# Inverse twiddle tables in quarters, the first layer norm's statistics inside inverse stage 1, two PSUM pools in inverse stage 2, and a new order of the front tables

## The chip, the cores and the metric

The kernel runs on one core of a Trainium2 chip. A core has a matrix engine (TensorE, in the profile PE, with its weight loads as PEld), VectorE (DVE), ScalarE (ACT), GpSimd (POOL) and SyncE (SP, which here only issues transfers). Every engine executes its own instructions in the order of the program; semaphores tie the engines together. SBUF is the working memory, PSUM the eight banks into which TensorE writes. The metric is the device time of one execution in microseconds (us); lower is better.

## The reference

Only what matters here: a causal long convolution with gating in front of a two-layer MLP, both with a layer norm ahead and a residual. S is 2048, D 512, DFF 1376; inputs and output are bf16.

```python
def _A_ref(q, k, v, shift_k, ssm_k, ssm_D):
    ...                                        # 4-tap causal filter of k, times v
    kv = k_shift * v
    kv_f = rfft(pad(kv, 2 * S)); kf_f = rfft(pad(ssm_k, 2 * S))
    y = irfft(kv_f * kf_f)[:S].astype(bfloat16)
    y = y + kv * ssm_D
    return q * y

x = A_q
h = x + _A_ref(_layernorm(x), A_k, A_v, A_shift_k, A_ssm_k, A_ssm_D)
h2 = h + relu(_layernorm(h) @ w1) @ w2
```

## The kernel before

The Fourier transforms are products with tables on TensorE, in two stages each way, with twiddle factors folded into the tables. The tables are made on the chip: an iota gives integers, `_turns` (L42) multiplies them by a column, adds an offset and takes the result modulo a power of two with an AND (two VectorE instructions), and a Sin on ScalarE makes the factor. The order of instructions on each engine is that of the program text (`manual_schedule`, L84); there is no scheduler.

The stages, one after another:

- *Front* (L94 to L193). The token-side inputs come by transposing transfers from SP. GpSimd makes the iotas, VectorE the turns and the diagonal tap weights `wdiag` (L172), ScalarE the Sins (`table`, L175). `c2s`, `c2c`, `c2n` are the tables of forward stage 2; `dre`, `dim` (L245, L275) those of inverse stage 1, from `dsc` (L243).
- *Forward stage 1* (L235 to L272). `to_rows` transposes the filter's rows on TensorE into PSUM, and copies alternate between ScalarE and VectorE; then eight rounds of `stage1` (small matmuls with `f1_hi`, `f1_lo`) and two `taps` each.
- *Forward stage 2, products* (L288 to L347). `spectrum_k`, then `product` and `finish`.
- *Inverse stage 1* (L394 to L408). Thirty-two steps `b`, each four matmuls of 128x256 into one of eight PSUM buffers, copied to `bp` by ScalarE or VectorE after the string in L404. Beside it run the transfers of the tokens `xh` (L356), `w1`, `w2`, and the inverse twiddles `ecore`: `ec_turns` in four parts at b = 0, 3, 10, 17 (GpSimd iota, two turns pairs on VectorE), `ec_sins` at b = 4, 12, 20, 28.
- *Inverse stage 2* (`inv2`, L419). Quarter q of the tokens uses `ecore` at n2 = 16a + 4q + l4, so that with `ecore` in four contiguous parts every quarter needs all four parts. Its matmuls are 32x32 tiles in fp32, each in two passes. The results go from PSUM tile `pz` to `zt` by ScalarE copies (L436).
- *Gate and second layer norm* (`gate`, L469; statistics, reciprocal root, normalisation on VectorE; the root for quarter 0 on ScalarE with Sqrt, L442, later ones on GpSimd, L446).
- *MLP.* Quarter 0 is transposed on TensorE (`transposes`, L517, PSUM `pt`, ScalarE copy to `hlnT`), the others by transposing transfers (L486). `mlp1` (L488) takes eleven groups of four matmuls into three PSUM buffers `ps1m`, each closed by a Relu on ScalarE; `mlp2` (L502) accumulates eleven matmuls and adds `xh` on VectorE.

At the seam between inverse stage 2 and the MLP the program text is L524 to L537: statistics and norm of quarter 0, then `inv2` and `gate` by halves of quarters 0 and 1 out of a pool `psZ0` of two `pz` buffers (all eight banks), then that pool is closed and `psT`, `psM`, `psZ` take its banks.

Of the kernel before, what the change touches and what calls it, by code (L numbers as in the profile page):

```python
# [56 lines left out]
def kernel(  # L57
# [25 lines left out]
    pl = _Pools(tc)  # L83
# [47 lines left out]
    def _sin(out, turns, M, neg=False):  # L131

        nc.scalar.activation(out=out, in_=turns, func=ACT.Sin, scale=(-TURN if neg else TURN) / M,
                             bias=(pbias if neg else nbias)[:])
# [10 lines left out]
    n2i = early.tile([P, 1], I32, name="n2i")  # L145
    for s in range(0, P, 64):
        nc.gpsimd.iota(n2i[s:s + 64, :], pattern=[[0, 1]], base=0, channel_multiplier=1)
    r2 = early.tile([P, 32, 64], I32, name="w_r")
    nc.gpsimd.iota(r2[:], pattern=[[2, 32], [128, 64]], base=1, channel_multiplier=0)
    r3 = early.tile([P, 64], I32, name="dm_r")  # L150
    nc.gpsimd.iota(r3[:], pattern=[[1, 64]], base=0, channel_multiplier=0)
    n1c = early.tile([P, 1], F32, name="n1c")
    n2c = early.tile([P, 1], F32, name="n2c")
    nc.vector.tensor_copy(out=n1c[:], in_=n1i[:])
# [7 lines left out]
    _sin(f1v[:, 0], t1[:, 0:32].rearrange("p (o k) -> p o k", o=8), 128)  # L162
    _sin(f1v[:, 1], t1[:, 32:64].rearrange("p (o k) -> p o k", o=8), 128, neg=True)


    cc = wp.tile([P, 32, P], F32R, name="c2c")
    cs = wp.tile([P, 32, P], F32R, name="c2s")
    cn = wp.tile([P, 32, P], F32R, name="c2n")
    tsn = early.tile([P, 32, 64], I32, name="w_ts")
    _turns(nc, tsn[:], r2[:], n2c[:], 8192, False)  # L170
    for rg in range(DC):
        nc.vector.tensor_tensor(out=wdiag[:, rg, :, :], in0=ident[:].unsqueeze(1).to_broadcast([P, KS, P]),  # L172
                                in1=wsh[:, rg, :].unsqueeze(2).to_broadcast([P, KS, P]), op=ALU.mult)

    def table(dst, turns, ks=slice(0, 32)):  # L175
        for dp in range(2):
# [1 line left out]
                                 scale=hsc[:, dp:dp + 1], bias=hbi[:, dp:dp + 1])  # L178

    table(cs, tsn)  # L180
# [6 lines left out]
    _turns(nc, r2[:], r2[:], n2c[:], 8192, True)  # L187
    dtab = consts.tile([P, 8, DC, 8], BF16, name="dtab")
    nc.gpsimd.tensor_copy(out=dtab[:], in_=d0[:].rearrange("p r (o g) -> p o r g", g=8))
    for h in range(4):  # L190
# [10 lines left out]
    def copy(eng, o, i):  # L201
        if eng == "A":
            nc.scalar.copy(out=o, in_=i)  # L203
        else:
            nc.vector.tensor_copy(out=o, in_=i)  # L205
# [31 lines left out]
    for q in range(8):  # L237
        to_rows(skv, q, kfl, "DADADADA"[q])

    t3 = early.tile([P, 2, 64], I32, name="dm_t")  # L240
    _turns(nc, t3[:, 0, :], r3[:], n2c[:], 64, True)
    _turns(nc, t3[:, 1, :], r3[:], n2c[:], 64, False)
    dsc = early.tile([P, 2, 64], F32, name="dm_f")  # L243
    _sin(dsc[:], t3[:], 64)
# [107 lines left out]

    late = pl.push("late", side="right")
    xh = late.tile([P, NT, D], BF16, name="xh")
    for a, src in enumerate(_tokens(x_d, 0, NT)):
        nc.sync.dma_start(out=xh[32 * a:32 * a + 32, :, :].rearrange("p t d -> p (t d)"), in_=src)  # L356
    w1 = late.tile([P, DC, DFF], BF16, name="w1")
    w2 = late.tile([P, NFC, D], BF16, name="w2")
    nc.sync.dma_start(out=w1[:], in_=B_w1.rearrange("(c p) f -> p c f", p=P))
# [18 lines left out]
    nc.vector.tensor_copy(out=k1o[:], in_=k1i[:])  # L378
    ect = {}

    def ec_turns(h):
        r4 = tmpc.tile([P, 16, 32], I32, tag="ec_r", name="ec_r", bufs=4)
        nc.gpsimd.iota(r4[:], pattern=[[1, 16], [64, 32]], base=16 * h, channel_multiplier=0)
        for quarter in (True, False):
            t = tmpc.tile([P, 16, 32], I32, tag=f"ec_t{quarter}", name="ec_t", bufs=2)
            _turns(nc, t[:], r4[:], k1o[:], 8192, quarter)
            ect[h, quarter] = t

    def ec_sins(h):
        hs = slice(16 * h, 16 * h + 16)  # L390
        _sin(ecore[:, 0, hs, :], ect[h, True][:], 8192)
        _sin(ecore[:, 1, hs, :], ect[h, False][:], 8192, neg=True)

    ec_turns(0)  # L394
    bp = slotA.tile([P, 64, 2, 2, 64], F32, tag="A", name="bp")
    for b in range(32):
        ps = psum.tile([P, 2, 2 * P], F32, tag="ps", name="psi1")
        m0 = 16 * (b % 4) + 2 * (b // 4)
        for i in range(2):
            m = 2 * b + i  # L400
            for c, d in ((0, dre), (1, dim)):
                nc.tensor.matmul(out=ps[:, i, :], lhsT=kf[:, c, 4 * m:4 * m + 4, :].rearrange("p r k -> p (r k)"),  # L402
                                 rhs=d[:].rearrange("p a b -> p (a b)"), start=(c == 0), stop=(c == 1))
        copy("ADAADADA"[b % 8], bp[:, m0:m0 + 2, :, :, :].rearrange("p g a b c -> p g (a b c)"), ps[:])  # L404
        if b in (3, 10, 17):
            ec_turns((b + 4) // 7)
        if b in (4, 12, 20, 28):
            ec_sins((b - 4) // 8)  # L408
    pl.pop("tmpc")
    pl.pop("slotB")  # L410
    pl.pop("psI")


    pzp = pl.push("psZ0", bufs=2, space=PSUM)
    ep = pl.push("ep", bufs=2)
    hp = pl.push("hp", bufs=2)
    zts, hlnTs, h1s = {}, {}, {}

    def inv2(q, l4s=(0, 1, 2, 3), between=None):  # L419
        pz = pzp.tile([P, 4, 4, P], F32, tag="pz", name="pz")  # L420
        for l4 in l4s:
            for rho in range(2):
                for a in range(4):
                    n2 = 16 * a + 4 * q + l4
                    for r4 in range(4):
                        rows = slice(32 * r4, 32 * r4 + 32)
                        rhs = bp[rows, :, rho, :, n2].rearrange("p (r g) d -> p r d g", r=DC)
                        nc.tensor.matmul(out=pz[32 * a:32 * a + 32, r4, l4, :], lhsT=ecore[rows, rho, n2, :], rhs=rhs,  # L428
                                         start=(rho == 0), stop=(rho == 1), tile_position=(32 * r4, 32 * a),
                                         skip_group_check=True)  # L430
            if between is not None:
                between(l4)
        if q not in zts:
            zts[q] = hp.tile([P, 4, D], BF16, tag="zt", name="zt")
        for l4 in l4s:
            nc.scalar.copy(out=zts[q][:, l4, :].rearrange("p (m r) -> p m r", r=4),  # L436
                           in_=pz[:, :, l4, :].rearrange("p r m -> p m r"))
# [10 lines left out]
    def stats(mv, ts):  # L448
        for t in ts:
            nc.vector.bn_stats(out=st[:, t % 4, :], in_=xh[:, t, :])  # L450
        for t in ts:
            nc.vector.bn_aggr(out=mv[:, t, :], in_=st[:, t % 4, :])  # L452
# [6 lines left out]
    def four(q):  # L459
        return [4 * q + i for i in range(4)]  # L460

    def ln1(q, on_act=False):
        stats(mv1, four(q))
        rstd(mv1, rstd1, four(q), on_act)
        qln = ep.tile([P, 4, D], BF16, tag="qln", name="qln")
        norm(qln, mv1, rstd1, four(q))
        return qln

    def gate(q, ts, qln, hln, on_act=False):  # L469
        for t in ts:  # L470
# [52 lines left out]

    qln = ln1(0, on_act=True)  # L524
    hln = new_rows(0)
    for ts in ([0, 1], [2, 3]):
        inv2(0, ts)
        gate(0, ts, qln, hln, on_act=True)
    for ts in ([0, 1], [2, 3]):
        inv2(1, ts)  # L530
    pl.pop("psZ0")
    ptp = pl.push("psT", bufs=1, space=PSUM)
    psum = pl.push("psM", bufs=3, space=PSUM)
    pzp = pl.push("psZ", bufs=1, space=PSUM)
# [7 lines left out]
    inv2(3, between=lambda i: mlp2(4 + i))  # L542
    chain(3, ln1(3))
    for sc in (2, 3):
        mlp1(sc)
# [33 lines left out]
```

## Time and profile before

| | |
|---|---|
| median of 5 executions | 234.16 us (234.05 to 234.85) |
| the profiled execution, its own time | 234.16 us |
| its span, first to last instruction | 232.4 us |
| mean granted TensorE clock | 0.97 |
| inverse stage 1 starts, first psi matmul | 101.83 us |
| inverse stage 2 starts, first pz matmul | 118.78 us |
| the first MLP matmul starts | 135.44 us |
| half clock in between | 130.5 to 140.8 us |

The span is 1.76 us shorter than the execution's own time. A line of a timeline gives the start in us, the length in us, the engine, the line of code, the operation with its operands, and in brackets how long the engine was idle before it and what released it. A line of the chain of waits gives start, length and what the end of the kernel hung on at that moment. "issue" is idle time for which the profile shows no wait.

### The profile page before, as it was taken

What the parts mean: (1) busy time and instruction counts of PE and PEld (TensorE: products, weight loads), DVE (VectorE), ACT (ScalarE), POOL (GpSimd) and SP (SyncE); (2) the same over time, 40 slices, a digit from 0 to 9 for tenths busy, and PEclk for the clock granted to TensorE, in tenths of its full rate; (3) what the DMA queues carried; (4) which work ended last, traced back from release to release, by engine and by line L of the source; (5) the groups of instructions that cost most, each with busy time, mean ns of one, the idle gap of its engine ahead of it and who ended that gap; (6) DMA issues with size and microseconds to landing.
All of it is one profiled execution on the core that took longest, in us unless ns stands there. A gap on an engine that the chain in (4) does not pass through costs nothing.

```text
span 232.4 us, 7243 instructions
## 1 busy us (share of the span) xinstructions
PE 204.9 (88%) x3092; PEld 143.0 (62%) x3111; DVE 156.1 (67%) x307; ACT 133.9 (58%) x252; POOL 58.4 (25%) x85
## 2 busy tenths in 40 slices
PE   0287998999988999989988689999999999989992
PEld 0284544989978999969975458744454544434451
DVE  6996989689987999959989976021595247740031
ACT  3765988678885888879973447502560056206500
POOL 6099500000016999970000022000102002200000
PEclk9997999999999999999999758999999999999999
DMA  5999920000000000059970000401101420042111
GB/s 183 293 223 182 173 61 4 0 4 3 6 3 3 1 0 0 3 109 212 292 242 3 6 0 9 84 25 41 29 3 29 82 65 13 0 96 60 28 45 45
DMA packets 30383, 15.45 MB, mean 67 GB/s; under 512 B 25648, under 2 KB 29200, under 8 KB 30224
## 3 DMA queue, kind: packets, MB, share of 16 engines
q1 hardware_dynamic: 29616, 14.87, 27.7%
q8 instruction: 24, 0.39, 0.7%
q10 hardware_dynamic: 736, 0.13, 0.3%
q14 instruction: 7, 0.06, 0.1%
HBM read 7.08 MB, written 2.10 MB: 40 GB/s over the span
## 4 chain that ended last, share of the span: by engine, by line
PE 56%; DVE 7%; ACT 2%; issue 1%; DMA 1%; DVEq 0%; SPq 0%; ACTq 0%
PE ps1m L498 18%; PE ps2m L510 15%; PE psi L402 7%; PE psy L338 5%; PE pz L428 5%; DVE st L450 3%; PE u L229 3%; PE u L231 3%; ACT kf L340 1%; DMA hlnT<-hln 1%; PE pt L521 1%; DVE t L328 1%; DVE hln L456 1%; DVE xh L473 1%; DVE qln L471 1%
## 5 line engine op out<-in xcount | busy, mean ns | idle before, releaser
L498 PE MATMUL ps1m<-hlnT,w 128*128 128x512 bf16 (+3 forms) x219 | 41.2, 351 | 2.3 <-ACT hlnT L522 1.2
L500 ACT ACTIVATE h1T<-ps1m 128x512 bf16<-128x512 f32 (+3 forms) x55 | 27.9, 511 | 25.3 <-PE ps1m L498 24.5
L512 DVE TENSOR_TENSOR o<-ps2m,xh 128x512 bf16<-128x512 f32 (+1 forms) x17 | 11.1, 658 | 45.7 <-PE ps2m L510 45.1
L510 PE MATMUL ps2m<-w,h1T 128*128 128x512 bf16 (+3 forms) x177 | 38.9, 366 | 0.7 <-issue 0.3
L498 PEld LDWEIGHTS <-w 128*128 128x128 bf16 (+1 forms) x220 | 22.9, 105 | 20.0 <-issue 2.8
L510 PEld LDWEIGHTS <-h1T 128*128 128x128 bf16 (+1 forms) x187 | 17.6, 98 | 21.2 <-issue 3.1
L328 DVE TENSOR_TENSOR t<-u,kf 128x704 fp32r<-128x704 f32 x32 | 26.7, 886 | 3.7 <-ACT usb L324 3.6
L328 POOL TENSOR_TENSOR t<-usb,kf 128x320 fp32r<-128x320 f32 x32 | 28.1, 915 | 2.1 <-ACT usb L324 1.7
L428 PE MATMUL pz<-bp,ecore 32*32 32x128 f32 x1024 | 23.0, 384 | 3.0 <-issue 2.0
L436 ACT CAST zt<-pz 128x512 bf16<-128x512 f32 x16 | 8.4, 591 | 26.9 <-PE pz L428 26.9
L445 POOL TENSOR_SCALAR rstd<-mv 128x4 f32<-128x4 f32 x6 | 1.4, 230 | 89.2 <-DVE mv L452 89.2
L428 PEld LDWEIGHTS pz<-bp,ecore 32*32 32x32 f32 x1024 | 14.6, 105 | 10.6 <-issue 6.5
L203 ACT CAST a<-ps 128x512 fp32r<-128x512 f32 x37 | 19.6, 591 | 2.3 <-PE ps L214 2.3
L450 DVE BATCH_NORM_STATS2 st<-xh 128x6 f32<-128x512 bf16 x32 | 19.8, 677 | 0.0
L205 DVE CAST a<-ps 128x512 fp32r<-128x512 f32 x27 | 17.6, 687 | 2.8 <-PE ps L214 2.8
L340 ACT CAST kf<-psy 128x512 fp32r<-128x512 f32 x32 | 18.3, 639 | 1.5
L402 PE MATMUL psi<-dre,kf 128*128 128x256 f32 x64 | 15.8, 288 | 0.8 <-ACT kf L340 0.8
L260 PE MATMUL pkv<-kT,wdiag 128*128 128x512 bf16 x56 | 15.7, 396 | 0.6 <-issue 0.2
L338 PE MATMUL psy<-t,ipos 128*128 128x512 f32 x48 | 15.8, 391 | 0.0
L198 PE MATMUL pst<-ident,sk 128*128 128x128 bf16 x64 | 6.6, 291 | 10.0 <-DMA sk<-in_A_ssm_k_dram 10.0
L402 PE MATMUL psi<-dim,kf 128*128 128x256 f32 x64 | 15.4, 283 | 0.0
L402 PEld LDWEIGHTS psi<-dre,kf 128*128 128x128 f32 x64 | 12.2, 191 | 1.6 <-ACT kf L340 1.3
(107 smaller groups left out, 386.2 us busy)
## 6 DMA issues: line engine op xcount, KB each, us to landing
sk<-in_A_ssm_k_dram SPq DMA_DIRECT2D x1, 2048.0 KB, 8.7
xh<-in_A_q_dram SPq DMA_DIRECT2D x4, 512.0 KB, 8.3
out_dram<-o SPq DMA_DIRECT2D x60, 32.0 KB, 1.6
w<-in_B_w_dram SPq DMA_DIRECT2D x1, 1376.0 KB, 15.4
w<-in_B_w_dram SPq DMA_DIRECT2D x1, 1280.0 KB, 18.4
hlnT<-hln SPq DMA_TRANSPOSE x12, 2.5
w<-in_B_w_dram SPq DMA_DIRECT2D x1, 96.0 KB, 18.1
d<-in_A_ssm_D_dram ACTq DMA_DIRECT2D x2, 32.0 KB, 5.8
```

The source lines that it names most:

```text
L203: nc.scalar.copy(out=o, in_=i)
L205: nc.vector.tensor_copy(out=o, in_=i)
L260: nc.tensor.matmul(out=ps[:], lhsT=wdiag[:, rg, j, :], rhs=kT[c][:, rg, 16 - j:CH + 16 - j], start=(j == 0), stop=(j == KS - 1))
L328: eng.tensor_tensor(out=t[:, :, j, :], in0=in0.unsqueeze(1).to_broadcast([P, 2, n, 2]), in1=kfr[:, :, j, ks], op=ALU.mult)
L338: nc.tensor.matmul(out=psy[:], lhsT=m_[:], rhs=t_.rearrange("p j k -> p (j k)"), start=first, stop=not first)
L340: nc.scalar.copy(out=kf[:, s, :, 2 * kp:2 * kp + 2], in_=psy[:].rearrange("p (j k) -> p j k", k=2))
L402: nc.tensor.matmul(out=ps[:, i, :], lhsT=kf[:, c, 4 * m:4 * m + 4, :].rearrange("p r k -> p (r k)"), rhs=d[:].rearrange("p a b -> p (a b)" ...
L428: nc.tensor.matmul(out=pz[32 * a:32 * a + 32, r4, l4, :], lhsT=ecore[rows, rho, n2, :], rhs=rhs, start=(rho == 0), stop=(rho == 1), tile_p ...
L450: nc.vector.bn_stats(out=st[:, t % 4, :], in_=xh[:, t, :])
L498: nc.tensor.matmul(out=ps1[:fsz, :], lhsT=w1[:, c, fc * P:fc * P + fsz], rhs=hlnTs[sc][:, c, part], start=(c == 0), stop=(c == DC - 1))
L500: nc.scalar.activation(out=h1s[sc][:fsz, fc, part], in_=ps1[:fsz, :], func=ACT.Relu)
L510: nc.tensor.matmul(out=ps2[:], lhsT=h1s[sc][:ksz, fc, i * P:(i + 1) * P], rhs=w2[:ksz, fc, ds], start=(fc == 0), stop=(fc == NFC - 1))
```

## The change

Five edits:

- *Front.* The small iota of the `dm` table comes before the large one; the `dm` turns and Sin move from after the filter's transposes to before the large turns; the `wdiag` products go from VectorE to GpSimd, ahead of `dtab` and `c2n`; the second large turns pair comes ahead of the Sins of `c2s` in the text.
- *Token loads.* Tiles 0 to 3 come in four transfers of their own, then tiles 4 to 15 in four.
- *Inverse twiddles.* The parts are now the quarters that `inv2` uses. Multiply and add are one GpSimd instruction per table and quarter, all issued ahead of inverse stage 1; the ANDs stay on VectorE. Quarters 0 and 1 get their ANDs and Sins at b = 8 and 16, quarters 2 and 3 after the first transposes of the MLP, ahead of the first Relu.
- *First layer norm.* The statistics of tiles 0 to 3 are taken tile by tile at b = 19, 22, 25, 28. The engines of the last two of every eight copies are exchanged.
- *Inverse stage 2.* Two pools of one `pz` each, of four banks. The copies to `zt` are a function of their own. The last pair of copies of quarter 1 stands after the first transposes; `psT` and `psM` take the banks of `psZA`.

```diff
+    r3 = early.tile([P, 64], I32, name="dm_r")
+    nc.gpsimd.iota(r3[:], pattern=[[1, 64]], base=0, channel_multiplier=0)
     r2 = early.tile([P, 32, 64], I32, name="w_r")
     nc.gpsimd.iota(r2[:], pattern=[[2, 32], [128, 64]], base=1, channel_multiplier=0)
-    r3 = early.tile([P, 64], I32, name="dm_r")
-    nc.gpsimd.iota(r3[:], pattern=[[1, 64]], base=0, channel_multiplier=0)
...
+    t3 = early.tile([P, 2, 64], I32, name="dm_t")
+    _turns(nc, t3[:, 0, :], r3[:], n2c[:], 64, True)
+    _turns(nc, t3[:, 1, :], r3[:], n2c[:], 64, False)
+    dsc = early.tile([P, 2, 64], F32, name="dm_f")
+    _sin(dsc[:], t3[:], 64)
...
-    for rg in range(DC):
-        nc.vector.tensor_tensor(out=wdiag[:, rg, :, :], in0=ident[:].unsqueeze(1).to_broadcast([P, KS, P]),
-                                in1=wsh[:, rg, :].unsqueeze(2).to_broadcast([P, KS, P]), op=ALU.mult)
...
     _turns(nc, r2[:], r2[:], n2c[:], 8192, True)
...
+    table(cs, tsn)
+    for rg in range(DC):
+        nc.gpsimd.tensor_tensor(out=wdiag[:, rg, :, :], in0=ident[:].unsqueeze(1).to_broadcast([P, KS, P]),
+                                in1=wsh[:, rg, :].unsqueeze(2).to_broadcast([P, KS, P]), op=ALU.mult)
...
-    for a, src in enumerate(_tokens(x_d, 0, NT)):
-        nc.sync.dma_start(out=xh[32 * a:32 * a + 32, :, :].rearrange("p t d -> p (t d)"), in_=src)
+    for ts in (slice(0, 4), slice(4, NT)):
+        for a, src in enumerate(_tokens(x_d, ts.start, ts.stop - ts.start)):
+            nc.sync.dma_start(out=xh[32 * a:32 * a + 32, ts, :].rearrange("p t d -> p (t d)"), in_=src)
...
+    def ec_product(q):
+        r4 = tmpc.tile([P, 4, 4, 32], I32, tag="ec_r", name="ec_r", bufs=2)
+        nc.gpsimd.iota(r4[:], pattern=[[16, 4], [1, 4], [64, 32]], base=4 * q, channel_multiplier=0)
+        ect[q] = [tmpc.tile([P, 4, 4, 32], I32, tag=f"ec_t{c}", name="ec_t", bufs=4) for c in range(2)]
+        for c in range(2):
+            nc.gpsimd.tensor_scalar(out=ect[q][c][:], in0=r4[:], scalar1=k1o[:], scalar2=(6144.0, 4096.0)[c],
+                                    op0=ALU.mult, op1=ALU.add)
+
+    def ec_table(q):
+        for c in range(2):
+            nc.vector.tensor_single_scalar(out=ect[q][c][:], in_=ect[q][c][:], scalar=8191, op=ALU.bitwise_and)
+        for c in range(2):
+            _sin(ecore[:, c].rearrange("p (a q l) n -> p q a l n", a=4, l=4)[:, q], ect[q][c][:], 8192, neg=c == 1)
+
+    def row_stats(mv, t):
+        nc.vector.bn_stats(out=st[:, t % 4, :], in_=xh[:, t, :])
+        nc.vector.bn_aggr(out=mv[:, t, :], in_=st[:, t % 4, :])
...
-        copy("ADAADADA"[b % 8], bp[:, m0:m0 + 2, :, :, :].rearrange("p g a b c -> p g (a b c)"), ps[:])
-        if b in (3, 10, 17):
-            ec_turns((b + 4) // 7)
-        if b in (4, 12, 20, 28):
-            ec_sins((b - 4) // 8)
+        copy("ADAADAAD"[b % 8], bp[:, m0:m0 + 2, :, :, :].rearrange("p g a b c -> p g (a b c)"), ps[:])
+        if b in (8, 16):
+            ec_table(b // 8 - 1)
+        if b in (19, 22, 25, 28):
+            row_stats(mv1, (b - 19) // 3)
...
-    pzp = pl.push("psZ0", bufs=2, space=PSUM)
+    pzB = pl.push("psZB", space=PSUM)
+    pzA = pl.push("psZA", space=PSUM)
...
-        stats(mv1, four(q))
+        if not on_act:
+            stats(mv1, four(q))
...
-    for ts in ([0, 1], [2, 3]):
-        inv2(0, ts)
-        gate(0, ts, qln, hln, on_act=True)
-    for ts in ([0, 1], [2, 3]):
-        inv2(1, ts)
-    pl.pop("psZ0")
+    t01, t23 = (0, 1), (2, 3)
+    inv2_copy(0, inv2(0, t01, pool=pzA), t01)
+    inv2_copy(0, inv2(0, t23, pool=pzB), t23)
+    gate(0, t01, qln, hln, on_act=True)
+    inv2_copy(1, inv2(1, t01, pool=pzA), t01)
+    gate(0, t23, qln, hln, on_act=True)
+    pz = inv2(1, t23, pool=pzB)
+    pl.pop("psZA")
     ptp = pl.push("psT", bufs=1, space=PSUM)
     psum = pl.push("psM", bufs=3, space=PSUM)
-    pzp = pl.push("psZ", bufs=1, space=PSUM)
     transposes(0, hln)
+    inv2_copy(1, pz, t23)
+    ec_table(2)
+    ec_table(3)
     mlp1(0, slice(0, 2 * P), lambda: transposes(2, hln))
...
-    inv2(2, between=mlp2)
+    inv2_copy(2, inv2(2, between=mlp2))
```

More of the change, by code (lines that the diff above doesn't have):

```diff
@@ L170 @@
     _turns(nc, tsn[:], r2[:], n2c[:], 8192, False)
-    for rg in range(DC):
-        nc.vector.tensor_tensor(out=wdiag[:, rg, :, :], in0=ident[:].unsqueeze(1).to_broadcast([P, KS, P]),
-                                in1=wsh[:, rg, :].unsqueeze(2).to_broadcast([P, KS, P]), op=ALU.mult)
-    def table(dst, turns, ks=slice(0, 32)):
-        for dp in range(2):
-            nc.scalar.activation(out=dst[:, ks, 64 * dp:64 * dp + 64], in_=turns[:, ks, :], func=ACT.Sin,
-                                 scale=hsc[:, dp:dp + 1], bias=hbi[:, dp:dp + 1])
-    table(cs, tsn)
     f1hi = consts.tile([P, 64], BF16, name="f1_hi")
@@ L187, with table @@
     _turns(nc, r2[:], r2[:], n2c[:], 8192, True)
+    def table(dst, turns, ks=slice(0, 32)):
+        for dp in range(2):
+            nc.scalar.activation(out=dst[:, ks, 64 * dp:64 * dp + 64], in_=turns[:, ks, :], func=ACT.Sin,
+                                 scale=hsc[:, dp:dp + 1], bias=hbi[:, dp:dp + 1])
+    table(cs, tsn)
+    for rg in range(DC):
+        nc.gpsimd.tensor_tensor(out=wdiag[:, rg, :, :], in0=ident[:].unsqueeze(1).to_broadcast([P, KS, P]),
+                                in1=wsh[:, rg, :].unsqueeze(2).to_broadcast([P, KS, P]), op=ALU.mult)
     dtab = consts.tile([P, 8, DC, 8], BF16, name="dtab")
@@ L238 @@
         to_rows(skv, q, kfl, "DADADADA"[q])
[L240 to L244, printed above, removed]
     dre = consts.tile([P, 2, P], F32R, name="dre")
@@ L379 @@
     ect = {}
[L381 to L394, printed above, removed]
+    def ec_product(q):
[13 more added lines that the diff above has]
+        nc.vector.bn_aggr(out=mv[:, t, :], in_=st[:, t % 4, :])
+    for q in range(4):
+        ec_product(q)
     bp = slotA.tile([P, 64, 2, 2, 64], F32, tag="A", name="bp")
@@ L403 @@
                                  rhs=d[:].rearrange("p a b -> p (a b)"), start=(c == 0), stop=(c == 1))
-        copy("ADAADADA"[b % 8], bp[:, m0:m0 + 2, :, :, :].rearrange("p g a b c -> p g (a b c)"), ps[:])
-        if b in (3, 10, 17):
-            ec_turns((b + 4) // 7)
-        if b in (4, 12, 20, 28):
-            ec_sins((b - 4) // 8)
-    pl.pop("tmpc")
+        copy("ADAADAAD"[b % 8], bp[:, m0:m0 + 2, :, :, :].rearrange("p g a b c -> p g (a b c)"), ps[:])
[3 more added lines that the diff above has]
+            row_stats(mv1, (b - 19) // 3)
     pl.pop("slotB")
     pl.pop("psI")
-    pzp = pl.push("psZ0", bufs=2, space=PSUM)
+    pzB = pl.push("psZB", space=PSUM)
+    pzA = pl.push("psZA", space=PSUM)
     ep = pl.push("ep", bufs=2)
@@ L417, with inv2 @@
     zts, hlnTs, h1s = {}, {}, {}
-    def inv2(q, l4s=(0, 1, 2, 3), between=None):
-        pz = pzp.tile([P, 4, 4, P], F32, tag="pz", name="pz")
+    def inv2(q, l4s=(0, 1, 2, 3), between=None, pool=None):
+        pz = (pool or pzB).tile([P, 4, 4, P], F32, tag="pz", name="pz")
         for l4 in l4s:
@@ L432, in inv2, with inv2_copy @@
                 between(l4)
+        return pz
+    def inv2_copy(q, pz, l4s=(0, 1, 2, 3)):
         if q not in zts:
@@ L538 @@
     chain(1, ln1(1))
-    inv2(2, between=mlp2)
+    inv2_copy(2, inv2(2, between=mlp2))
     chain(2, ln1(2))
     mlp1(1)
-    inv2(3, between=lambda i: mlp2(4 + i))
+    inv2_copy(3, inv2(3, between=lambda i: mlp2(4 + i)))
     chain(3, ln1(3))
```

## The prediction

> **What bounds the kernel now.** I read the shares first, then the chain of waits in order of time, then one engine's timeline for each stretch that the change touches.
>
> ```profile
> PE 204.9 (88%) x3092; PEld 143.0 (62%) x3111; DVE 156.1 (67%) x307; ACT 133.9 (58%) x252; POOL 58.4 (25%) x85
> ```
>
> PE leads by far, but the mean hides the stretches without it. The chain of waits (start, length, what) shows the longest:
>
> ```profile
> 117.99 2.46 DVE st L450 x4
> ...
> 130.87 2.39 DVE st L450 x4
> 133.28 1.02 PE pt L521 x8
> 134.38 1.02 ACT hlnT L522
> 135.44 4.42 PE ps1m L498 x20
> 139.87 0.85 PE pt L521 x8
> 140.72 7.66 PE ps1m L498 x68
> 148.38 1.39 PE pz L428 x62
> ```
>
> From 117.5 to 135.4 us the chain runs through the layer norm and the gate on DVE, then transposes, a copy and the first MLP. From 148.4 on it is PE almost to the end, so a delay or gain before 148.4 passes through one for one. PE's own timeline says that DVE is not alone:
>
> ```profile
> 118.78 4.43 PE L428 MATMUL pz<-bp,ecore 32*32 32x128 f32 x210 [0.96 <-ACT bp L203]
> 123.61 2.75 PE L428 MATMUL pz<-bp,ecore 32*32 32x128 f32 x128 [0.40 <-issue]
> 126.90 2.75 PE L428 MATMUL pz<-bp,ecore 32*32 32x128 f32 x127 [0.54 <-issue]
> 130.73 1.38 PE L428 MATMUL pz<-bp,ecore 32*32 32x128 f32 x47 [1.08 <-issue]
> 133.28 1.01 PE L521 MATMUL pt<-ident,hln 128*128 128x128 bf16 x8 [1.16 <-DVE st L450]
> ```
>
> Call the start of inverse stage 2 S (118.78). Its 512 records break every 128 at "issue", not at a tile's border, and 16 KB packets of the instruction queue land about 1 us after each restart: PE waits for its own instructions. These matmuls and their order stay, so I keep their length, S to S+13.3, whatever DVE does. The wait before pt is named after DVE; ACT's timeline shows the true one, two zt copies that end at 133.22 in the PSUM which psT takes over:
>
> ```profile
> 132.15 1.07 ACT L436 CAST zt<-pz 128x512 bf16<-128x512 f32 x2 [1.29 <-PE pz L428]
> 134.38 1.01 ACT L522 COPY hlnT<-pt 128x1024 bf16<-128x1024 bf16 x1 [1.15 <-PE pt L521]
> 136.49 0.38 ACT L500 ACTIVATE h1T<-ps1m 128x256 bf16<-128x256 f32 x1 [1.10 <-PE ps1m L498]
> ```
>
> ACT is idle after that, so the first Relu costs the MLP nothing. The windows (slice, its length, busy us and count of PE, PEld, DVE, ACT and POOL, then the granted clock) show the clock: half from 130.5 to 140.8 us, which is why 20 matmuls of 256 columns take 4.42 us (0.88 for a group of four) and the later 68 take 7.66 (0.45).
>
> ```profile
> 129.00:130.00 1.00, 0.65 (x31) 0.20 (x17) 0.64 (x4) 0.39 (x2) 0.00 (x0) 1.00 0.00 0
> 131.00:132.00 1.00, 1.00 (x47) 0.54 (x18) 1.00 (x3) 0.00 (x0) 0.00 (x0) 0.50 0.08 16
> 141.00:142.00 1.00, 1.00 (x11) 0.90 (x10) 0.73 (x5) 1.00 (x3) 0.18 (x1) 1.00 0.00 0
> ```
>
> The prices that I use, from the groups:
>
> ```profile
> L192 POOL TENSOR_SCALAR c2n<-c2s 128x1024 fp32r<-128x1024 f32 x4 | 11.3, 2844 | 1.0 <-ACT c2s L177 1.0
> L133 ACT ACTIVATE ecore<-ec_t,nbias 128x512 f32<-128x512 int32 x4 | 3.0, 742 | 0.0
> L442 ACT ACT_TABLE_LOAD x1 | 1.3, 1283 | 0.0
> ```
>
> **What the Trainium skill says.** "ScalarE: Activation LUTs", section "What ACT_TABLE_LOAD costs": 1283 ns for a switch of table set, and some 1380 ns of drain behind it. The trace agrees on 1283; the drain it can't show, since ACT waited for DVE after both loads. "TensorE: Matmul & The Clock Gate", "What's actually happening": half or full clock is granted by windows of 3.4 us of PE activity. Agrees: the half clock lasted 10.24 us, three windows; a window some 79% busy (17.9 to 21.3) brought the clock back, one 65% busy (133.9 to 137.4) did not. "SBUF — State Buffer", "Who interferes with whom": a VectorE operation in a 2-port mode and a GpSimd one exclude each other for a whole instruction. Agrees only in part: VectorE's 128x2048 AND took 2.02 us beside a GpSimd c2n product and 1.23 without, slower but not shut out for that product's 3.06.
>
> **The change, part by part.**
>
> *Front.* VectorE loses wdiag (2.49 us) and makes the small dm turns first (0.9). GpSimd gains four wdiag products; nearest is its 128x320 product at 0.915 us, so 512 elements are 1.46 each, 5.9 in all, from 4.6 to 10.5 us, beside VectorE's w_ts pair. With the 2.02/1.23 slowdown w_ts ends near 10.4 instead of 7.5; ScalarE's c2s (4.2) then ends at 14.6 instead of 11.7 and its four kfl copies (3.8 back to back) at 18.4; before they waited for PE and ended at 17.7. VectorE's second table ends near 13.4, and its kfl copies at 18.0 instead of 18.4. PE's stage 1 began at 18.59, behind VectorE; now near 18.4, behind ScalarE. It runs at half clock there, so I take -0.1. Best is 17.7 (PE's last transpose plus a copy): -0.9. If each small VectorE operation waits out a whole product, as the 32-element f1 turn did beside the 2048-element iota (1.94 us against 0.23), c2s slips to 18.7 and stage 1 to 22.7: +4. c2n moves from 23 to 26-30 us, and is wanted at 46: nothing.
>
> *Inverse stage 1.* PE needs 128 matmuls by 0.12 from 101.83, to 117.6. ScalarE loses four Sins (4 by 0.64), which had made it end at 118.73: it now ends by 117.6. VectorE loses eight turns pairs (8.2 us) and gains four ANDs and four row statistics (0.68+0.15 each). GpSimd gains eight products: by L192 1.4 us for 512 elements, with a 0.68 iota per quarter: quarters are ready at 105.3, 108.8, 112.3, 115.8. The first AND is due at 106.2, the third at 110.4, after b=15: no wait. From there VectorE has two ANDs at 0.8 (GpSimd is busy beside them; 0.43 alone), six copies by 0.62, four statistics by 0.83: 8.6, to 119.0. So VectorE takes ScalarE's place and S becomes 118.3 to 119.1; I take +0.1. The product is multiply and add on integers, which no row shows: below 1.4 I see no reason; at twice that (2.8, two passes) the second quarter is ready at 114.4, behind it stand VectorE's copies and ScalarE's Sins, PE runs out of PSUM at b=25, and S is 122.2: +3.5.
>
> The token loads are split in two, four more SP issues by 0.44 us: w1 and w2 slip by 1.8 and are wanted at 135 and 150. The first quarter is wanted at 111. Nothing.
>
> *Inverse stage 2 and the MLP's start.* Statistics of quarter 0 leave (2.46+0.36 on VectorE). But PE can't use it: S+13.3 stands by instruction supply, and hln of tiles 0-1 is due at S+8.4. VectorE's gate waits for ScalarE, which now copies zt of tiles 2-3 (PE ends them at S+6.1) before the rstd: 0.7 later, hidden. With psZA freed by an earlier copy, pt no longer waits for the last zt (1.16): transposes S+13.4 to 14.4, copy to S+15.5, first ps1m at S+15.5 instead of S+16.66. That is the gain, -1.15.
>
> Behind that copy ScalarE now has, in its order of program: two zt (1.0), a table load (1.28), four Sins (3 by 0.64 + 0.7 = 2.6), and only then the first Relu: S+20.4 to S+20.75. Their ANDs are done by S+14.2, so ScalarE is the late one. psM has three buffers: PE does three groups (2.65 at half clock, to S+18.15) and stands until S+20.8. Before, its fourth group began at S+19.3. The gain is gone and 1.5 us are lost.
>
> The stall also spoils the clock: 2.65 us without PE in S+18.15 to 20.8. If windows lie as in this trace (borders at S+18.6, 22.0, 25.4), the first full one ends at S+25.4, not S+22.0. From S+20.8: two groups at 0.88, transposes 0.85, 2.2 groups more by 25.4, then 14.8 groups by 0.45: S+32.05. Before: 148.38, or S+29.6. So +2.4. Windows run freely: clock back at 23.4 gives +1.5, at 26.8 +3.2; the drain behind the table load would add up to 1.4. Without any half clock it is 20.8 + 19 by 0.45 + 0.5 = S+29.9: +0.3.
>
> *Sum.* -0.1 + 0.1 + 2.4 = +2.4 on the profiled execution's 234.16 us (span 232.4), which is also the median: 236.5.
>
> **Rivals.**
> A, the forecast, ScalarE's backlog before the first Relu: 236.5.
> B, faster: the grant of the clock. If PE is not at half clock when the MLP restarts, the stall is nearly paid by the earlier start (+0.3), and what ScalarE is spared in stage 1 (-0.5, with ANDs at 0.43) and the front (-0.5) remain: 233.5. It decides at a clock back before S+21. For it: transposes now follow pz at once. Against it: a 2.65 us hole in which a window must fall below 79%.
> C, slower still: the integer products on GpSimd take over 2.2 us and hold stage 1: 234.16 + 2.4 + up to 3.5, say 239. For it: GpSimd's rate in L192 is already 2.7 ns an element. Against: it streamed that one in a single pass.
> D: the port in the front, VectorE shut out by wdiag: 240. For it the f1 turn; against it the AND at 2.02.
> E: gains and stall cancel (clock back at 23.4, S at 118.3, stage 1 of the front at 17.7): 234.2.
>
> **Numbers.** A 0.51, B 0.17, C 0.18, D 0.08, E 0.06. So faster by over 0.2% (0.47 us, about what a measurement here can tell) 0.17, within it 0.06, slower 0.77. The range: below to B's 233.5, above to C and D, 240.0. A's own range is 235.2 to 238.2.
>
> **What would show it.** ScalarE's timeline: table load and four Sins between the hlnT copy and the first Relu, PE idle some 2.7 us after its twelfth ps1m matmul; half clock until about S+25; pt within 0.2 us of the last pz. In stage 1 VectorE, not ScalarE, releases the first pz. GpSimd's products near 1.4 us. The front's stage 1 near 18.4. I am wrong if the first Relu isn't held, if the half clock ends as early as before, or if S moves by over 1 us.

## The result, and the profile after

| | before | after |
|---|---|---|
| median of the runs | 234.26 us | 236.74 us (234.01 to 238.32, 26 runs) |
| ratio, 95% interval | | 1.0079 (1.0057 to 1.010) |
| profiled execution, its own time | 234.16 us | 237.71 us |
| its span, mean granted clock | 232.4 us, 0.971 | 235.9 us, 0.964 |
| start of forward stage 1 on PE | 18.59 | 19.27 |
| start of inverse stage 1 | 101.83 | 104.48 |
| start of inverse stage 2, S | 118.78 | 120.97 |
| first MLP matmul | S+16.66 | S+15.07 |
| end of the first MLP part | S+29.53 | S+30.66 |

The medians differ by 2.48 us (1.06%); the ratios, here and below, leave out slow runs, more than 1.5% above the fastest of their kernel (ten of after's), while the medians are of all runs. The profiled executions differ by 3.55 us: after's profile is one of its longer executions, so the stretches below are compared one by one. How much of a run goes at half clock varies, and time follows it: after's runs lie between 234.01 us at a mean clock of 0.993 and 238.32 at 0.954.

After's page, first lines of the shares (engine, busy us and share of the span, instructions): PE has done the same work, VectorE has lost 12 instructions and GpSimd gained 12.

```profile
PE 205.4 (87%) x3092; PEld 143.9 (61%) x3111; DVE 152.6 (65%) x295; ACT 135.1 (57%) x253; POOL 69.3 (29%) x97
```

After's chain of waits at the seam (start, length, what the end hung on; pieces under 0.1 us are left out):

```profile
132.95 1.38 PE pz L436 x44
134.32 0.58 PE pt L533 x8
134.98 1.01 ACT hlnT L534
135.99 0.98 ACT zt L447 x2
136.99 1.28 ACT L133
138.28 2.56 ACT ecore L133 x4
140.84 0.28 ACT h1T L512
141.16 1.86 PE ps1m L510 x8
143.02 0.85 PE pt L533 x8
143.88 7.82 PE ps1m L510 x68
151.70 1.39 PE pz L436 x62
```

Before, this stretch of the chain was VectorE's statistics, the transposes, one copy, and from then on PE alone. Now VectorE has left it, pt follows pz at once, and for 6.2 us the end hangs on ScalarE: hlnT copy, two zt copies, the table load (L133 without a tile), four Sins, the first Relu. PE's timeline of after shows what that costs (in brackets idle time and its releaser):

```profile
134.26 0.63 PE L533 MATMUL pt<-ident,hln 128*128 128x128 bf16 x8
136.04 1.47 PE L510 MATMUL ps1m<-hlnT,w 128*128 128x256 bf16 x12 [1.16 <-ACT hlnT L534]
141.16 1.86 PE L510 MATMUL ps1m<-hlnT,w 128*128 128x256 bf16 x8 [3.65 <-ACT h1T L512]
```

Twelve matmuls, three PSUM buffers, then 3.65 us of nothing. And the windows of after (the number after POOL's is the granted clock) show that PE stood at full clock and was at half once it went on:

```profile
138.00:139.00 1.00, 0.00 (x0) 0.00 (x0) 0.06 (x1) 0.99 (x3) 0.91 (x1) 1.00 0.00 0
142.00:143.00 1.00, 1.00 (x7) 0.73 (x6) 1.00 (x5) 0.38 (x1) 0.00 (x0) 0.50 0.00 0
145.00:146.00 1.00, 1.00 (x12) 0.90 (x10) 0.67 (x5) 0.95 (x3) 0.23 (x1) 1.00 0.00 0
```

In narrower windows half clock lies at 130.9 to 134.3 and again at 141.1 to 144.6; from 137.7 to 141.1, a stretch of the same 3.4 us, PE did nothing. Before, it lay at 130.7 to 141.0.

In inverse stage 1, GpSimd's timeline of after has the integer products in pairs, VectorE's has the ANDs in pairs, and PE's has the releaser of the first pz:

```profile
105.36 1.48 POOL L388 TENSOR_SCALAR ec_t<-ec_r,k1o 128x512 int32<-128x512 int32 x2
112.41 1.88 POOL L388 TENSOR_SCALAR ec_t<-ec_r,k1o 128x512 int32<-128x512 int32 x2
```
```profile
109.22 1.16 DVE L393 TENSOR_SCALAR ec_t<-ec_t 128x512 int32<-128x512 int32 x2
113.06 0.75 DVE L393 TENSOR_SCALAR ec_t<-ec_t 128x512 int32<-128x512 int32 x2
```
```profile
120.97 4.41 PE L436 MATMUL pz<-bp,ecore 32*32 32x128 f32 x210 [0.88 <-DVE bp L210]
```

A product takes 0.74 to 0.94 us in the mean of a pair, an AND 0.58 and 0.38, and VectorE, not ScalarE, is last. In the front, two of VectorE's small turns in before and its stage 1 on PE:

```profile
18.37 0.27 DVE L44 TENSOR_SCALAR dm_t<-dm_r,n2c 128x64 int32<-128x64 int32 x1
18.67 0.20 DVE L46 TENSOR_SCALAR dm_t<-dm_t 128x64 int32<-128x64 int32 x1
```
```profile
18.59 0.24 PE L214 MATMUL ps<-f_hi,kfl 32*128 32x64 bf16 x4 [1.93 <-DVE kfl L205]
```

And GpSimd's, VectorE's and PE's timeline of after:

```profile
4.57 4.03 POOL L191 TENSOR_TENSOR wdiag<-ident,wsh 128x512 bf16<-128x512 bf16 x4
```

```profile
5.55 1.09 DVE L44 TENSOR_SCALAR dm_t<-dm_r,n2c 128x64 int32<-128x64 int32 x1
6.68 0.96 DVE L46 TENSOR_SCALAR dm_t<-dm_t 128x64 int32<-128x64 int32 x1
7.57 1.08 DVE L44 TENSOR_SCALAR dm_t<-dm_r,n2c 128x64 int32<-128x64 int32 x1
8.68 0.20 DVE L46 TENSOR_SCALAR dm_t<-dm_t 128x64 int32<-128x64 int32 x1
```
```profile
19.27 0.24 PE L219 MATMUL ps<-f_hi,kfl 32*128 32x64 bf16 x4 [2.63 <-ACT kfl L208]
```

Instructions that took 0.20 to 0.27 us before take about 1 us, until 8.6, when GpSimd's four wdiag products end; the fourth, behind that, has its old 0.20. Stage 1 begins 0.68 us later than before, released by ScalarE.

### The profile page after: what moved, and what is told of

It reads as the page before. It is cut to its first block, busy times and chain, and to the rows that moved or that the text cites. A ratio compares the mean times of both kernels' runs of the same rounds, so it can differ in the third digit from the quotient of the medians.

```text
span 235.9 us, 7247 instructions
## 1 busy us (share of the span) xinstructions
PE 205.4 (87%) x3092; PEld 143.9 (61%) x3111; DVE 152.6 (65%) x295; ACT 135.1 (57%) x253; POOL 69.3 (29%) x97
## 4 chain that ended last, share of the span: by engine, by line
PE 59%; ACT 4%; DVE 2%; issue 2%; DMA 1%; SPq 0%; ACTq 0%
PE ps1m L510 16%; PE ps2m L522 15%; PE pz L436 10%; PE psi L410 5%; PE psy L338 5%; PE u L234 4%; PE u L236 4%; ACT kf L340 1%; ACT ecore L133 1%; DMA hlnT<-hln 1%; DVE bp L210 1%; PE pt L533 1%; ACT L133 1%; DVE st L398 1%; DVE o L524 0%
## 5 line engine op out<-in xcount | busy, mean ns | idle before, releaser
L510 PE MATMUL ps1m<-hlnT,w 128*128 128x512 bf16 (+3 forms) x219 | 40.3, 344 | 6.0 <-ACT h1T L512 3.6
L510 PEld LDWEIGHTS <-w 128*128 128x128 bf16 (+1 forms) x220 | 22.4, 103 | 23.2 <-issue 6.7
L436 PEld LDWEIGHTS pz<-bp,ecore 32*32 32x32 f32 x1024 | 14.7, 106 | 10.4 <-issue 6.5
L461 DVE BATCH_NORM_STATS2 st<-xh 128x6 f32<-128x512 bf16 x28 | 17.3, 677 | 0.0
L260 PE MATMUL pkv<-kT,wdiag 128*128 128x512 bf16 x56 | 16.5, 415 | 0.6 <-issue 0.2
L410 PE MATMUL psi<-dre,kf 128*128 128x256 f32 x64 | 15.5, 284 | 0.7 <-ACT kf L340 0.7
L263 DVE TENSOR_TENSOR vT<-pkv,vT 128x512 bf16<-128x512 f32 x16 | 10.8, 689 | 3.4 <-PE pkv L260 3.3
```

Of the source, the lines that this page charges most:

```text
L260: nc.tensor.matmul(out=ps[:], lhsT=wdiag[:, rg, j, :], rhs=kT[c][:, rg, 16 - j:CH + 16 - j], start=(j == 0), stop=(j == KS - 1))
L510: nc.tensor.matmul(out=ps1[:fsz, :], lhsT=w1[:, c, fc * P:fc * P + fsz], rhs=hlnTs[sc][:, c, part], start=(c == 0), stop=(c == DC - 1))
```

## The experiments

**The two halves of the change alone.** e1 is the kernel before with the front of after; e2 is after with the front of before.

```diff
 e1, on before (e2 has the same hunks backwards, on after)
+    r3 = early.tile([P, 64], I32, name="dm_r")
+    nc.gpsimd.iota(r3[:], pattern=[[1, 64]], base=0, channel_multiplier=0)
     r2 = early.tile([P, 32, 64], I32, name="w_r")
...
+    t3 = early.tile([P, 2, 64], I32, name="dm_t")
+    _turns(nc, t3[:, 0, :], r3[:], n2c[:], 64, True)
+    _turns(nc, t3[:, 1, :], r3[:], n2c[:], 64, False)
...
-        nc.vector.tensor_tensor(out=wdiag[:, rg, :, :], ...
+        nc.gpsimd.tensor_tensor(out=wdiag[:, rg, :, :], ...
```

> The kernel before with the new front alone. If the loss comes mostly from ScalarE's backlog ahead of the first Relu, this costs only what the front's profile shows: forward stage 1 starts at 19.3 us instead of 18.6, +0.7 (up to +1.7 if the half clock lasts a window longer there): 234.9 to 236. If the front carries the whole loss: 236.7. If the front's delay is absorbed later: 234.2.

> The changed kernel with the front of before. Backlog theory: PE still stands 2.7 to 3.7 us after the third group of the first MLP and the total stays slower than before, 235 to 236. If the front carries the loss: 233.5 to 234.3, not slower than before.

Measured: e1 235.37 us (22 runs), ratio 1.0061 (1.0034 to 1.0087); e2 235.80 (22 runs), 1.0066 (1.0040 to 1.0092), where before gave 234.39. Both fall where the explanation by ScalarE's queue expected them, and each half costs something by itself. The medians put the front at 1.0 us and the rest at 1.4, together the whole change's 2.4; the ratios put them at 1.4 and 1.5, against 1.9 for the whole. The intervals, 0.8 to 2.0 us and 0.9 to 2.2, allow either, so the split is known only roughly. In their profiles forward stage 1 starts at 19.33 in e1 and 18.57 in e2: the front's part is that 0.7, and from there to inverse stage 1 e1 takes 83.1 us as before did (83.2). After took 85.2 for the same instructions. That part of its profile is the clock's, not the change's: the five profiles on record (after, e4, e7, e9, e10) that have a stretch of half clock between 70.8 and 76.3 us take 84.6 to 85.5 there, and the other eight take 83.1 to 84.0. Both groups have kernels with the new front and with the old.

**The Sins off the seam.** e3 is after with the tables of quarters 2 and 3 ahead of the first layer norm; e4 is e3 with the front of before. All of the computation stays.

```diff
+    ec_table(2)
+    ec_table(3)
     qln = ln1(0, on_act=True)
...
     inv2_copy(1, pz, t23)
-    ec_table(2)
-    ec_table(3)
     mlp1(0, slice(0, 2 * P), lambda: transposes(2, hln))
```

> The changed kernel, with the four late Sins (and their ANDs) moved ahead of the first Sqrt, so that no table load and no Sin stands between the hlnT copy and the first Relu. Backlog theory: PE's stand after the third group shrinks from 3.65 us to under 0.3; the gate on VectorE comes some 3.7 us later, which the instruction-bound matmuls of inverse stage 2 hide; total 2 to 2.5 us below the changed kernel: 234.3. If PE's stand has another cause (PSUM, the transposed rows), it stays: 236.7. If the late gate isn't hidden, the transposes wait for hln and the gain is under 1 us.

> Both: the front of before and the four Sins ahead of the first Sqrt. Backlog theory: what is left of the change is the earlier transposes (-1.15) and a stage 1 some 0.4 us shorter: 232.5 to 233.3, faster than before. If these two are hidden by something else: 234.2.

> The version with the Sins of quarters 2 and 3 ahead of the first layer norm once more, with more rounds than before. The first measurement gave a ratio of 0.987 on six runs; if that was the effect and not the phase of the clock, it is again 0.983 to 0.992 of the kernel before (231 to 232.5 us where that one takes 234.4). If it was the phase, it lies at 0.995 or above.

Measured: e3 231.38 us (6 runs), 0.9869 (0.9814 to 0.9924); e4 231.85 (6 runs), 0.9882 (0.9824 to 0.9940); e11, the same kernel as e3, 233.71 (22 runs), 0.9943 (0.9910 to 0.9976), beside a before of 234.74. The six runs of e3 came out some 3 us below their expectation, 234.3, and those of e4 below theirs, 232.5 to 233.3. The second measurement is outside the window that was set for "effect" (0.983 to 0.992) and below the one for "phase" (0.995): the six runs had a higher mean clock (0.980 against e11's 0.973), which accounts for a part of the difference, and about 0.6% is what stands. The six runs of e4 are to be read with the same reserve. Against after's 1.0079, e11 is some 3.2 us better (1.36% of 234.4), for moving two lines. PE's timeline of e11:

```profile
131.91 0.62 PE L533 MATMUL pt<-ident,hln 128*128 128x128 bf16 x8
133.68 2.34 PE L510 MATMUL ps1m<-hlnT,w 128*128 128x256 bf16 x20 [1.16 <-ACT hlnT L534]
135.86 0.61 PE L533 MATMUL pt<-ident,hln 128*128 128x128 bf16 x8
136.31 7.82 PE L510 MATMUL ps1m<-hlnT,w 128*128 128x256 bf16 x68
```

Twenty matmuls run through where after stood after twelve, at full clock (2.34 us; 4.42 before, at half). The part ends at S+24.93 here and at S+28.15 in e3's profile, whose clock was half from 128.7 to 139.0.

**The size of the backlog.** e5 is after with the four Sins issued twice, the second time with the same result; e6 takes the roots of quarter 0 on GpSimd instead of ScalarE, so that no Sqrt stands between Sins and the table load goes.

```diff
 e5
     ec_table(3)
+    for q in (2, 3):
+        for c in range(2):
+            _sin(ecore[:, c].rearrange(...)[:, q], ect[q][c][:], 8192, neg=c == 1)
 e6
-        rstd(mv1, rstd1, four(q), on_act)
+        rstd(mv1, rstd1, four(q), False)
...
-        rstd(mv2, rstd2, ts, on_act)
+        rstd(mv2, rstd2, ts, False)
```

> The changed kernel with the four late Sins done twice (same output), which doubles the suspected cost. Backlog theory: PE's stand after the third group of the first MLP grows from 3.65 us by four Sins of 0.63, to 6.2, and the total by 2.5 to about 239.2. If ScalarE is not the late one there, both stay: 3.65 and 236.7.

> The changed kernel with the reciprocal roots of quarter 0 on GpSimd, so that neither the Sqrt nor the second Sin table load is needed. Backlog theory: the stand shrinks by one table load of 1.28 us, from 3.65 to 2.37 us, and the total by 1.3 to about 235.4. If a drain behind the load counts too: by up to 2.7. If only the Sins matter: no change.

Measured: e5 239.47 us (4 runs), ratio 1.0199 (1.0151 to 1.0246); e6 235.21 (20 runs), 1.0027 (0.9997 to 1.0057), both beside a before of 235.03 and both near what was expected. PE's timeline of e5, then of e6:

```profile
134.64 2.72 PE L510 MATMUL ps1m<-hlnT,w 128*128 128x256 bf16 x12 [1.16 <-ACT hlnT L534]
142.20 1.87 PE L510 MATMUL ps1m<-hlnT,w 128*128 128x256 bf16 x8 [4.84 <-ACT h1T L512]
```
```profile
134.98 2.60 PE L510 MATMUL ps1m<-hlnT,w 128*128 128x256 bf16 x12 [1.16 <-ACT hlnT L534]
138.68 1.87 PE L510 MATMUL ps1m<-hlnT,w 128*128 128x256 bf16 x8 [1.10 <-ACT h1T L512]
```

The bracket alone misleads: it is 4.84 where 6.2 was expected, because the twelve matmuls ran at half clock and took 2.72 instead of 1.47. Read from the first ps1m to the fourth group it is 7.56 us in e5, 5.12 in after and 3.70 in e6: plus 2.44 for four Sins, minus 1.42 for a table load. (In e9, below, it is 4.14, less by the two zt copies' 0.98.) So the backlog passes to PE one for one, and what stands on PE is ScalarE's sum, whatever the clock. ScalarE's timeline of after and of e6 gives the load its price:

```profile
135.89 1.08 ACT L447 CAST zt<-pz 128x512 bf16<-128x512 f32 x2
136.99 1.28 ACT L133 ACT_TABLE_LOAD   x1
138.28 0.72 ACT L133 ACTIVATE ecore<-ec_t,nbias 128x512 f32<-128x512 int32 x1
```
```profile
134.83 1.08 ACT L447 CAST zt<-pz 128x512 bf16<-128x512 f32 x2
135.78 0.74 ACT L133 ACTIVATE ecore<-ec_t,nbias 128x512 f32<-128x512 int32 x1
```

The load starts 0.02 us after the end of the copies ahead of it, and the Sin 0.01 us after the load's end.

**The earlier start of the MLP.** e9 is after, e10 is e3, each with the last two zt copies ahead of the transposes.

```diff
+    inv2_copy(1, pz, t23)
     transposes(0, hln)
-    inv2_copy(1, pz, t23)
```

> The changed kernel with the last two zt copies of quarter 1 ahead of the transposes in the text, so that ScalarE makes them before the hlnT copy, as the kernel before did. If the prediction's gain of 1.15 us (first ps1m earlier) is swallowed whole by ScalarE's backlog, the first ps1m comes 0.4 to 0.6 us later after the start S of inverse stage 2 (15.5 to 15.7 instead of 15.07), the first Relu stays at S+19.8, and the stand of PE before the fourth group shrinks by what the start slips: end of the first MLP part and time as the changed kernel's, 236.5 to 237. If the copy order does decide something, everything behind it moves by the same 0.5 us: 237.2.

> The version with the Sins of quarters 2 and 3 ahead of the first layer norm, and with the zt copies ahead of the transposes. Here no backlog stands before the first Relu, so an earlier start should be worth its length: first ps1m at S+16.3 to 16.5 instead of S+15.9, and the time 0.4 to 0.6 us above that version's run beside it. If the start of the MLP isn't on the path, both are equal within 0.2 us.

Measured: e9 236.86 us (4 runs), ratio 1.0107 (1.0051 to 1.0163); e10 233.31 (19 runs), 0.9907 (0.9872 to 0.9943), beside e11's 233.71; before gave 234.74. In e9's PE timeline

```profile
136.56 2.72 PE L510 MATMUL ps1m<-hlnT,w 128*128 128x256 bf16 x12 [1.16 <-ACT hlnT L534]
140.70 1.87 PE L510 MATMUL ps1m<-hlnT,w 128*128 128x256 bf16 x8 [1.42 <-ACT h1T L512]
```

the first ps1m is at S+15.50, 0.43 later than in after as expected, and yet the fourth group comes at S+19.64, 0.55 *earlier*, against the expectation that the Relu stays: ScalarE began its zt copies while PE was still transposing, instead of waiting for pt first. The part ends at S+30.24, after's at S+30.66, and the times agree (2.1 us above the before beside it, after 2.5). So the early start of the MLP is worth nothing while the backlog stands. e10 missed: without the backlog the later start was to cost 0.4 to 0.6 us, and it came out 0.4 below e11, within what the runs' spread (230 to 236 us) can tell. Its first ps1m, at S+15.18, was early beside e3's S+15.91 and late beside e11's S+14.55. And its chain of waits names another path than the expectation had: the Sins at 121.26, the first layer norm behind them, the gate, its last root on ScalarE, the zt copies.

```profile
121.26 2.52 ACT ecore L133 x4
...
133.66 0.23 DVE mv L463 x2
133.88 0.02 issue
133.91 0.30 ACT rstd L453
134.21 0.90 ACT zt L447 x2
```

With the Sins ahead, the gate is about as late as PE, and the zt copies stand behind its root. What the early start is worth by itself stays open.

**The two edits of the front.** e7 is e4 with the wdiag products on GpSimd, in their old place; e8 is e4 with the small iota and the dm turns early, wdiag on VectorE.

```diff
 e7
-        nc.vector.tensor_tensor(out=wdiag[:, rg, :, :], ...
+        nc.gpsimd.tensor_tensor(out=wdiag[:, rg, :, :], ...
 e8
+    r3 = early.tile([P, 64], I32, name="dm_r")
+    nc.gpsimd.iota(r3[:], pattern=[[1, 64]], base=0, channel_multiplier=0)
     r2 = early.tile([P, 32, 64], I32, name="w_r")
...
+    _turns(nc, t3[:, 0, :], r3[:], n2c[:], 64, True)
+    _turns(nc, t3[:, 1, :], r3[:], n2c[:], 64, False)
+    dsc = early.tile([P, 2, 64], F32, name="dm_f")
+    _sin(dsc[:], t3[:], 64)
     cc = wp.tile([P, 32, P], F32R, name="c2c")
```

> e4 with one part of the new front: wdiag on GpSimd, the dm turns late as before. If it is the port that costs (small VectorE turns each wait out one wdiag product of 1.0 us), two or three f1 turns wait, the large turns pair begins near 7 instead of 5 us, c2s ends near 14, and forward stage 1 starts at 18.2 to 18.6 us (18.57 with the front of before): no loss. If GpSimd's products alone delay it as much as the whole new front does: 19.3.

> e4 with the other part of the new front: the dm turns and iota early, wdiag on VectorE as before. Without a GpSimd product beside them the four turns cost 0.9 us and delay c2s by as much, while VectorE's later work comes 0.9 earlier and later by the same: forward stage 1 starts near 18.6. If the early turns alone are the delay: 19.3.

Measured: e7 232.97 us (15 runs), ratio 0.9864 (0.9826 to 0.9902); e8 232.54 in one run, which as a time says little. GpSimd's and VectorE's timeline of e7, PE's of e7, and PE's of e8:

```profile
4.54 5.03 POOL L172 TENSOR_TENSOR wdiag<-ident,wsh 128x512 bf16<-128x512 bf16 x4
```
```profile
4.60 1.02 DVE L44 TENSOR_SCALAR f_t<-f_r,n1c 128x32 int32<-128x32 int32 x1
6.54 2.13 DVE L44 TENSOR_SCALAR w_ts<-w_r,n2c 128x2048 int32<-128x2048 int32 x1
8.70 1.94 DVE L46 TENSOR_SCALAR w_ts<-w_ts 128x2048 int32<-128x2048 int32 x1
```
```profile
18.61 0.21 PE L214 MATMUL ps<-f_hi,kfl 32*128 32x64 bf16 x4 [1.31 <-ACT kfl L203]
```
```profile
19.21 0.24 PE L219 MATMUL ps<-f_hi,kfl 32*128 32x64 bf16 x4 [2.44 <-DVE kfl L210]
```

wdiag on GpSimd alone is even, as expected: what VectorE loses beside it (a small turn at 1.02 instead of 0.23, the large pair at 4.07 instead of 2.51) it is spared by the 2.49 us of products, and stage 1 starts at 18.61. The large pair loses by the same waiting as the small turns, once for each of its two instructions. Its first runs from 6.54, when the third product begins, to 8.67; in turn the fourth product, begun at 7.55, takes 2.02 us instead of 1.04 and ends at 9.57, and the second of the pair, from 8.70, takes 1.94 instead of 1.23.

For e8 the expectation was 18.6, and 19.3 if the early turns alone are the delay: they are, at 19.21. They put 0.9 us ahead of everything that VectorE does before its kfl copies, which then end at 19.06 instead of 18.44. Beside 18.57 in e4, the two edits bring 0.04 and 0.64 us, and both together, in e3 with the same rest, 0.70: they add up. In after the turns meet the products (c2s and kfl times from the timelines of ScalarE and VectorE). ScalarE's table of `c2s` comes late (11.37 to 15.60, before 7.53 to 11.70), its kfl copies end at 19.21 and are the last, and VectorE's end at 19.11, hardly sooner.

## Why the prediction was right, and where it was not

The time (236.5, measured 236.74) and the main cause hold, but that the totals agree so closely is in part luck. Of the three terms of the sum, -0.1 for the front, +0.1 for inverse stage 1 and +2.4 for the seam, the profiles show +0.7, -0.5 and +1.1: two have the wrong sign, and the third is half as large. They add up to +1.3, where the medians differ by 2.5 and the ratio gives 1.9; the rest is not placed.

*ScalarE's backlog before the first Relu: right, and shown.* The order hlnT, two zt, table load, four Sins, Relu is in the chain of after word for word, and three experiments move it as a cause must: away in e3 and e11, longer in e5, shorter in e6. The stand was put at 2.65 us and is 3.65, since the three groups before it ran at full clock (1.47 for 2.65); the backlog's end, S+20.75 in the prediction, is S+20.19. The drain of up to 1.4 us behind the table load, which the forecast left in its range, isn't there: the Trainium skill's "ScalarE: Activation LUTs", section "What ACT_TABLE_LOAD costs", has 1283 ns and a drain of 1380. Here the load took its 1.28 us, no gap of that size stands before or behind it (0.02 and 0.01 us), and its removal brings 1.42 in all.

*The clock after the stall: right in kind, too large in size.* Half clock was to last from before the seam to S+25.4, and cost 2.4 us by S+32.05. In after it lay at 130.9 to 134.3, was full while PE stood, and was half again for 3.4 us from 141.1, to S+23.6; the part ended at S+30.66. So the seam's term is +1.1 in that profile, and +1.2 between e1 (S+28.83) and e2 (S+30.01), not +2.4. It is near the forecast's own second case, clock back at S+23.4 for +1.5, which the sum did not take. By the medians it would be nearer 1.9, e2's +1.4 less the -0.46 of stage 1, with the wide interval of e2. That the stall brings the half clock is likely: in after and e2 the 3.4 us ahead of it had 0.00 and 0.21 us of work on PE, and all five profiles with the backlog (after, e2, e5, e6, e9) are at half when PE goes on (eight matmuls in 1.86 or 1.87 us). But half clock at this place comes without the stall too, in e3. The forecast's shares, 79% busy to bring the clock back and 65% not, give no threshold: stretches of 3.4 us with PE 60% busy were followed by full clock in after (134.3 to 137.7) and by half in e6 (131.8 to 135.2). Before and during the wait the clock hardly matters, because a slower PE only waits less there: in e9, where half clock lay at 134.1 to 144.4 through the whole wait, the part ended at S+30.24.

*Rival B: it did not come.* It took full clock at the seam as what would pay for the stall. None of the five profiles with the backlog has full clock when PE goes on, so that case was not measured. What was measured speaks against it: without the backlog full clock ends the part at S+24.93 (e11) and half clock at S+27.83 to 28.15 (e4, e3). Set beside the forecast's own estimate for a stall at full clock, S+29.9, the backlog would cost 5 us there, more than at half. Of B's other gains, stage 1 came (-0.46 for -0.5), and the front did not (+0.7 for -0.5).

*The gain of the transposes: right and worthless.* pt follows pz at once, and the first ps1m came at S+15.07 (S+15.5 predicted). e9 shows that while the backlog stands nothing of it arrives.

*Inverse stage 2, S+13.3: right.* pz ends at S+13.36, with its gaps again at "issue" (0.44, 1.08, 0.48 us). The gaps vary: over the profiles of all runs the end lies between S+12.85 and S+13.79, so differences of some tenths of a us at the seam between two profiles mean little.

*Inverse stage 1: wrong in sign, -0.46 for +0.1.* It shows in every profile: 16.95 and 17.08 us in before and e1, 16.48 or 16.49 in all the others. That VectorE takes ScalarE's place is right. The term that was too large is that of VectorE's last two ANDs, priced at 0.8 each for a busy GpSimd beside them and measured at 0.38. They came just as a product ended, and it was the next product that took longer (1.10 us for 0.69). With that the 8.6 us from the third AND to VectorE's last copy became 7.8. The products too were priced too high, 1.4 us by L192 for 0.74 to 0.94, but they were on no path, as forecast. Of the Trainium skill, "GPSIMD Engine Reference", section 3.1, has 769 ns measured for 512 elements as its best case, which would have been the nearer price; the row of the profile was for another type (fp32r out of f32). Rival C, slow integer products, fell by the same number.

*The front: wrong in sign.* Predicted -0.1, measured +0.68 at the start of stage 1 and about +1.0 in e1's median. The step that failed is the price of moving the dm turns ahead: 0.9 us, set off against wdiag. In after three of the four had to wait out a wdiag product of 1.0 us each, so that they took 3.2 us (5.55 to 8.79) and the large pair behind them ended at 11.33, where 10.4 was forecast. ScalarE's kfl copies then ended at 19.21 for 18.4, and VectorE's at 19.11 for 18.0. That waiting is rival D's mechanism, and the Trainium skill's "SBUF — State Buffer", section "Who interferes with whom", has it: of a VectorE operation in a 2-port mode and a GpSimd one the first to issue holds the shared ports for its whole length. The traces agree for the wdiag products, with small turns (0.20 to 0.27 became 0.95 to 1.09) and, in e7, with the large pair and the fourth product; whether these turns run in a 2-port mode, no run shows. D's +4 was far too much, as its price was a 1.46 us product; the products took 1.0 and were over at 8.6. And the waiting is not the only way to lose: in e8, where no product stands beside the early turns but VectorE keeps wdiag, they cost 0.64.

*What is not shown.* Per run, half-clock time can be read as (1 - mean clock) x 2 x span; after's profile has 17.0 us by it. It was 14.3 us on average in after's runs, and 10.8, 11.6 and 12.4 in the three sets of before's runs beside the experiments. Within the runs of one kernel time rises by 0.15 to 0.19 us per us of it (before, after, e1, e2, e6; 0.28 in e7, e10 and e11). So by estimate 0.3 to 0.6 us of the 2.5 goes with more half clock (1.9 to 3.5 us, times 0.17 to 0.18). Whether the change causes that, or the phase of the windows, no experiment here separates: of the kernels with the backlog e2 had 11.3 us and e6 16.6.

## What to carry to other kernels

Before work is moved to where an engine "is idle", list what that engine has behind it in its own order, and how many buffers the next engine may fill meanwhile: here three PSUM buffers made a 5 us queue on ScalarE into a 3.65 us stand of PE. The same four Sins cost little 17 us earlier, where PE's instruction supply set the pace, although e10 shows that even there they all but reach the path through the gate: e11, at 0.9943 (0.9910 to 0.9976) of before, and with the old front and wdiag on GpSimd e7, at 0.9864 (0.9826 to 0.9902), beat both kernels. And when work is to be hidden from one engine on another, look at what the two do to each other: moving wdiag to GpSimd freed 2.49 us of VectorE and gained nothing. Last, a forecast whose total agrees can still have terms wrong in sign; only running the halves alone shows it.

## What the runs showed of the hardware

- A table load of 1.28 us with no drain visible: 0.02 us ahead of it, the Sin 0.01 us after its end, 1.42 us saved where it goes (after, e6).
- VectorE's integer turns beside GpSimd's bf16 products wait out a product each, the small ones (0.95 to 1.09 us for 0.18 to 0.27) like the large ones (2.13 for 1.28, 1.94 for 1.23), and a product behind a large turn waits in the same way (2.02 for 1.04); after and e7 show it. Beside the fp32r scaling of c2n a large AND of before took 2.02 for 1.23, and did not wait out its 3.06.
- GpSimd's price depends on the form: 0.74 us for an int32 multiply-add of 512 elements where VectorE is not in its way, 1.03 for a bf16 product of two tensors of 512, 2.77 for an fp32r scaling of 1024 (after).
- Half clock came in stretches of 3.4, 6.8, 10.2 or 17.1 us, apart from a shorter one at the end of the span. PE 60% busy for 3.4 us was followed by full clock in one profile (after) and by half in another (e6).
- Runs of one kernel lie up to 4.3 us apart, more than the whole change, and follow the mean clock (after: 234.01 us at 0.993, 238.32 at 0.954); six runs of e3 and 22 of the same kernel in e11 differed by 2.3 us in their medians.
